# Attention sums of two query blocks in one session, and a head laid in another order, in a fused transformer block

## The chip, the cores and the metric

The kernel runs on one core of one Trainium2 chip. The metric is the device time of one execution in microseconds (us), the median of several runs; before the change it is 978.51 us over 3 runs. The engines are TensorE (PE; its weight loads are shown apart as PEld), VectorE (DVE), ScalarE (ACT), GpSimd (POOL) and SyncE (SP), which issues most transfers.

## The reference

One block of a transformer on x of 2048 tokens by 640 channels, in 32-bit floating point, whose norms are modulated by a condition c. Cut to what matters:

```python
mod = (_silu(c) @ w_mod).reshape(c.shape[0], 6, 1, -1)
sa, ca, ga, sb, cb, gb = (mod[:, i] for i in range(6))
h = _layernorm(x) * (1 + ca) + sa
x = x + ga * attention(h, wqkv, wo)        # 32 heads of 20, causal, window of 256 tokens
h = _layernorm(x) * (1 + cb) + sb
x = x + gb * mlp(h)                        # layernorm, 640 -> 1536, gelu, 1536 -> 640
```

A query sees the 256 keys up to and with its own, so in blocks of 128 tokens a query block meets three key blocks: its own and the one two back are masked to a triangle, the one between is whole.

## The kernel before, in words

The large products (projections, wo, MLP) are made of three matmuls each: the operands are split into a high part that TensorE multiplies fast (fp32r) and a low part, the rest; high by high, low by high and high by low are added in PSUM. A w_hi is a copy, a w_lo or hlo a subtraction. One line of the profile covers nearly all instructions, L116, the helper that keeps them in the order in which they are written: every engine works its own list in program order, and waits where a semaphore says so.

**The head** goes up to the first scores. It loads c (as columns, and as a row spread over all partitions, silr), x of the first 512 tokens (xs0), the first weights, the 640 columns' modulation weights wc in five pairs, x of the next 512 (xs1), the table sel and the constant rows of two key buffers (ones_k). All of these are issued on SP's queue, in that order but for the place of xs1 between the second and third pair. Then ORDER, a string, lays out the work: T turns a tile of 128 channels of a chunk of 512 tokens (transposes on TensorE, modulation and high part on ACT), L makes its low part (on POOL if it is in LOWP, else on DVE), P does its six matmuls, M computes a column pair of the modulation (sa, ca): on TensorE if it is in PE_COLS, else by eight multiply-and-sum operations on DVE and three small ones. S are statistics of a block of xs1, N normalizes xs1, R are matmuls without use that keep TensorE going, RUN0 as many ahead of all, E evacuates a product, Y lays it into the score buffers.

**The attention loop** has one iteration t for each of 128 score items (2 halves of the tokens, 8 quads of four heads, 8 query blocks) and some more to drain. In iteration t, TensorE does in this order: the exponent's scores e of the item 11 iterations back (LAG; keys by queries), the scores s of item t (queries by keys, for the row maximum), the sums o (exponent times v) of the query block that is due, and then a share of the projections pp that a planner has laid into four slots of the iteration, with asides (transposes, small sums) between. DVE masks e, masks s and takes its maximum nm; ACT copies the sums from PSUM (oT), takes the exponent pt; POOL makes the two triangular parts of pt by masking copies. The sums of a query block lie PVLAG iterations behind the e that completes it. ACT's queue then stores each second oT to o_scr. The sums, the turned tiles and the other asides share one PSUM bank, tag o.

The planner lay_units spreads the matmuls of 54 projection units over the iterations up to 108: an even room for each, less what else the iteration holds, where EXTRA[t] shifts the running total at t by so many matmuls. EARLY, AFTER, SUMS_LAST, WHOLE and the lists of times place single steps. From about iteration 115 on the blocks of 128 tokens that are done go through mid_steps: o scaled and split, wo, the first residual, the norm, its modulation, the transposes for the MLP. norm1 applies mean and deviation on ACT, mod multiplies by cb and adds sb in two halves, on DVE or on POOL. The rest of the blocks is done inside the MLP that follows.

What the steps touch: pv_stage, pv_copy and pv_store (the sums), pv_at (where they lie), lay_units, norm1 and mod in mid_steps, turned_in and modulate in the head, and the loads ahead of ORDER.

Of the kernel before, what the change touches and what calls it, by code (L numbers as in the profile page):

```python
# [31 lines left out]
PVLAG = 2  # L32
RUN0 = 33
PE_COLS = (0, 2)
PARTS = 4
MODV = 133
WOL = [1, 1, 0, 0, 0]
ORDER = ('T00 M1 L00 S0 S1 S2 T01 R8 S3 L01 P00 R5 N M2 R4 T02 M3 P01 T03 R2 L02 R1 T10 L10 L03 R6 C T11 M4 P02 T04 L11 P10 L04 T12 L12 T13 P03 P11 P04 L13 E0 T14 L14 Y00 P12 P13 Y01 P14')
LOWP = ['L00', 'L11', 'L03', 'L10', 'L13', 'L12', 'L04']
# [29 lines left out]
MODS = [[8.75, 17.0], [18.75, 27.0], [70.25, 79.0]]
WOS = [89.75, 94.0, 99.5, 109.0, 111.75, 114.25, 117.5]  # L70
W1S = [117.75, 121.75, 133.75]
RS = [[79.5, 82.5], [86.0, 87.0]]
# [1420 lines left out]
```

## Time and profile before

| What | us |
|---|---|
| Three runs | 977.36, 978.51, 978.64 |
| Median | 978.51 |
| Span of the profiled execution, first to last instruction | 975.4 |
| TensorE busy in it | 945.9 (97%) |
| DVE, ACT, POOL busy | 589.0, 445.1, 487.8 |
| First scores, start of the attention loop's work | 48.5 |

For the profiled execution the page gives its span; the time of the runs includes 2.0 to 3.2 us that lie outside it, by the difference. A row of a group of instructions reads: line, engine, operation, output <- inputs, shapes, count, then busy time and the mean of one in ns, then idle time of the engine ahead of them and what ended it. A row of a timeline reads: start, length, engine, line, operation, tiles, shapes, count. Matmuls are pipelined and their ends are modelled, so of two in a row the distance of the starts tells what one costs.

### The profile page before, as it was taken

How to read it: one execution, taken by the hardware profiler on the slowest of the kernel's cores; microseconds unless marked ns; L12 is line 12 of the kernel's file. 1: busy time of each engine (PE TensorE's matmuls, PEld its weight loads, DVE VectorE, ACT ScalarE, POOL GpSimd, SP SyncE). 2: the span in 40 equal slices, each digit the busy share in tenths (PEclk: the TensorE clock that was granted, in tenths of full speed). 3: DMA queues.
4: the chain of work that ended last, by engine and by line, in shares of the span. 5: the costliest groups of instructions: out<-in, count | busy, mean ns of one | idle time of the engine just before them, and what ended most of it. 6: DMA issues, size and time to landing. Idle time of an engine off the chain costs nothing.

```text
span 975.4 us, 20091 instructions
## 1 busy us (share of the span) xinstructions
PE 945.9 (97%) x7781; PEld 751.9 (77%) x7781; DVE 589.0 (60%) x991; ACT 445.1 (46%) x781; POOL 487.8 (50%) x674
## 2 busy tenths in 40 slices
PE   8899999999999999999889999999999999999998
PEld 8777777777777777777677677888888888888886
DVE  6564977888776786767788556563544344342112
ACT  3723555666654545555545654434333243333222
POOL 3423555677864364463646844654454454332121
PEclk9999999999999999999999999999999999999999
DMA  8366778666778359854862245444413342124113
GB/s 307 97 210 197 244 228 274 188 187 170 220 226 251 114 175 283 240 157 120 226 161 76 81 142 156 127 130 138 138 57 103 115 145 85 54 58 144 54 43 119
DMA packets 98974, 152.17 MB, mean 156 GB/s; under 512 B 8864, under 2 KB 42112, under 8 KB 98880
## 3 DMA queue, kind: packets, MB, share of 16 engines
q1 hardware_dynamic: 89664, 142.50, 48.4%
q10 hardware_dynamic: 9216, 8.39, 2.7%
q8 instruction: 62, 1.02, 0.4%
q14 instruction: 32, 0.26, 0.1%
HBM read 98.51 MB, written 51.58 MB: 154 GB/s over the span
## 4 chain that ended last, share of the span: by engine, by line
PE 81%; DVE 7%; ACT 5%; DMA 2%; issue 2%; POOL 1%; SPq 1%; ACTq 0%; DVEq 0%; POOLq 0%
PE pp L116 17%; PE out L116 16%; PE h L116 16%; PE e L116 8%; PE o L116 7%; PE wo L116 6%; PE s L116 4%; ACT pt L116 3%; DVE e L116 2%; PE ppo L116 1%; SPq L116 1%; PE yt L116 1%; DVE nm L116 1%; DMA wc<-in_wcol 1%; PE xt L116 1%
## 5 line engine op out<-in xcount | busy, mean ns | idle before, releaser
L116 POOL TENSOR_SCALAR_AFFINE_SELECT pt<-pt 128x512 f32<-128x512 f32 x192 | 129.1, 672 | 128.8 <-ACT pt L116 122.0
L116 ACT ACTIVATE pt<-e 128x1024 f32<-128x1024 f32 (+1 forms) x120 | 133.7, 1114 | 64.5 <-DVE e L116 62.0
L116 DVE TENSOR_REDUCE nm<-s 128x1 f32<-128x256 f32 (+4 forms) x206 | 157.6, 796 | 4.4
L116 POOL TENSOR_TENSOR w2lo<-w2r,w2hi 128x640 fp32r<-128x640 f32 x48 | 78.5, 1635 | 163.0 <-ACT w2hi L116 163.0
L116 PE MATMUL e<-qbuf,kbuf 62*128 62x128 f32 (+2 forms) x773 | 111.8, 328 | 10.6 <-ACT pt L116 9.5
L116 DVE CAST ghi<-g 128x512 fp32r<-128x512 f32 x48 | 27.4, 571 | 155.0 <-ACT g L116 155.0
L116 PEld LDWEIGHTS e<-qbuf,kbuf 62*128 62x128 f32 x773 | 80.8, 185 | 49.8 <-ACT pt L116 25.9
L116 PE MATMUL pp<-hhi,w_hi 128*128 128x512 f32 x265 | 113.6, 429 | 0.2 <-ACT pf L116 0.2
L116 PE MATMUL s<-kbuf,qbuf 60*128 60x384 f32 (+2 forms) x728 | 105.9, 302 | 4.3 <-DVE nm L116 1.9
L116 PE MATMUL pp<-hlo,w_hi 128*128 128x512 f32 x265 | 108.3, 409 | 0.6 <-POOL hlo L116 0.6
L116 DVE COPY_PREDICATED e<-mask_t,e 128x512 f32<-128x512 uint32 x96 | 66.6, 694 | 70.0 <-PE e L116 65.8
L116 PE MATMUL pp<-hhi,w_lo 128*128 128x512 f32 x265 | 106.2, 401 | 0.0
L116 PE MATMUL o<-pt,vbuf 128*32 128x128 f32 x2688 | 99.6, 277 | 0.6 <-ACT xT L116 0.6
L116 PEld LDWEIGHTS s<-kbuf,qbuf 60*128 60x128 f32 x728 | 89.1, 186 | 14.2 <-DVE nm L116 5.9
L116 PE MATMUL out<-ghi,w2hi 128*128 128x512 f32 x240 | 95.3, 397 | 0.9 <-ACT g L116 0.9
L116 PE MATMUL out<-glo,w2hi 128*128 128x512 f32 x240 | 93.9, 391 | 0.0
L116 PE MATMUL out<-ghi,w2lo 128*128 128x512 f32 x240 | 93.8, 391 | 0.0
L116 POOL TENSOR_TENSOR w_lo<-wraw,w_hi 128x128 fp32r<-128x128 f32 x171 | 76.1, 476 | 31.4 <-ACT w_hi L116 31.4
L116 PE MATMUL h<-yhi,w1hi 128*128 128x512 f32 x220 | 87.6, 398 | 0.0
L116 PE MATMUL h<-ylo,w1hi 128*128 128x512 f32 x220 | 86.1, 392 | 0.0
L116 PE MATMUL h<-yhi,w1lo 128*128 128x512 f32 x220 | 86.0, 391 | 0.0
L116 DVE COPY_PREDICATED s<-mask_t,s 128x512 f32<-128x512 uint32 x112 | 77.1, 688 | 13.8 <-PE s L116 13.5
(179 smaller groups left out, 1838.3 us busy)
## 6 DMA issues: line engine op xcount, KB each, us to landing
w2r<-in_w SPq DMA_DIRECT2D x48, 320.0 KB
qbuf<-q_scr SPq DMA_DIRECT2D x60, 240.0 KB
wraw<-in_wqkv SPq DMA_DIRECT2D x36, 320.0 KB
kbuf<-k_scr SPq DMA_DIRECT2D x44, 240.0 KB
q_scr<-stage SPq DMA_DIRECT2D x20, 512.0 KB
k_scr<-stage SPq DMA_DIRECT2D x20, 512.0 KB
o_scr<-oT ACTq DMA_DIRECT2D x64, 128.0 KB
wm<-in_wmod SPq DMA_DIRECT2D x20, 320.0 KB
```

What stands on the lines that cost most here:

```text
L116: return self.tc.keep_in_program_order(op(*args, **kw))
```

## The change: what it does

Sums: pv_stage does two query blocks in one session, into one bank as two columns blocks; one copy brings both to SBUF and one store follows. A pair b of a quad lies at u = min(2b + 1, 6) + half, one iteration (PVLAG = 1) behind its last e, so that in eight iterations four have sums, where each had before. SPOT names iterations whose sums are done in a later slot, behind projections. The planner counts PV_COST = 2 matmuls for an iteration with sums, and EXTRA has other values.

Head: x's tiles are asked for first; c goes on ACT's queue; the stores of constant rows come ahead of the last column pairs; LOADS is the order. M1 joins M0 and M2 on TensorE, RUN0 goes from 33 to 21, the R entries from 26 in sum to 1. ORDER, LOWP and HIGHV (high parts on DVE instead of ACT) are laid anew.

Second norm: norm1 goes; mod works on all 640 columns, first (x - mean) times cb, then times the deviation plus sb, both on DVE. WLV names units whose next weights' low parts are made on DVE instead of POOL.

UNITS, LNS, LOV, HIA, EARLY, AFTER, SUMS_LAST, WHOLE, MODS, WOS, W1S, RS, WARM, LATE_AT, TAIL0, TAIL_AT, MID_AT and CHAIN have some other values (CHAIN without norm1), which the diff leaves out.

```diff
-PVLAG = 2
-RUN0 = 33
-PE_COLS = (0, 2)
+PVLAG = 1
+RUN0 = 21
+PE_COLS = (0, 1, 2)
...
-MODV = 133
-ORDER = ('T00 M1 L00 S0 S1 S2 T01 R8 S3 L01 P00 R5 N M2 R4 T02 M3 P01 T03 R2 L02 R1 T10 L10 L03 R6 C T11 M4 P02 T04 L11 P10 L04 T12 L12 T13 P03 P11 P04 L13 E0 T14 L14 Y00 P12 P13 Y01 P14')
-LOWP = ['L00', 'L11', 'L03', 'L10', 'L13', 'L12', 'L04']
+ORDER = 'T00 L00 S0 M1 T01 S1 L01 S2 R1 P00 S3 M2 T02 N M3 P01 T03 T10 L02 L10 C L03 T11 M4 T04 P02 L04 P10 T13 T12 P03 P04 L11 P11 E0 L12 L13 Y00 T14 P12 L14 Y01 P13 P14'
+LOADS = 'x0 x1 c1 x3 x2 w1 r0 w0 m0 m1 y0 y1 o m2 m3 s m4'
+HIGHV = ['H03', 'H13', 'H14', 'H12']
+LOWP = ['L00', 'L10', 'L01', 'L03', 'L02', 'L12']
...
-MV = [8, 9, 12, 17, 19, 21, 22, 26, 28, 29, 30]
+WLV = [0, 12, 14, 15, 18, 28, 29, 33, 47, 49, 57, 59]
+SPOT = {99: 3, 40: 3, 44: 3, 128: 2, 115: 1, 118: 1, 69: 2, 54: 3, 119: 3, 107: 3, 11: 3, 45: 3, 51: 3, 14: 2, 109: 1, 123: 2, 111: 3, 89: 3, 76: 3}
...
+PV_COST = 2.0
-EXTRA = {9: -2, 10: -3, 11: 5, 14: -4, 15: 3, 16: -4, 17: 2, 18: 1, 19: -3, 20: -4, 21: 6, 22: 1, 23: 1, 25: 4, 26: -3, 27: 3, 28: -3, 29: 7, 30: -5, 31: 1, 32: -3, 33: -1, 34: -1, 35: -3, 36: 3, 37: 9, 38: -8, 39: 3, 40: -3, 41: -8, 42: -2, 43: 3, 44: -3, 45: 9, 46: 3, 47: -1, 48: 4, 50: 1, 51: -3, 52: -16, 53: 7, 54: -5, 55: 4, 56: -7, 57: 13, 58: -1, 59: 10, 60: -1, 61: 3, 63: 2, 64: -1, 65: 10, 66: -4, 67: -1, 69: 2, 70: -4, 71: 4, 72: 3, 73: 3, 75: -9, 76: -2, 77: -3, 78: -1, 79: -1, 80: -4, 81: -9, 82: 15, 83: 6, 84: -2, 85: 2, 86: 2, 87: 11, 88: 4, 89: -9, 90: 3, 91: 1, 92: 3, 93: -6, 94: -12, 95: 1, 96: 1, 98: 3, 99: 2, 100: 2, 101: 7, 102: -3, 103: 6, 104: -4, 105: -1, 106: -6, 107: -2, 108: -1, 109: 7, 110: 1, 111: 3, 112: 4, 114: -1}
+EXTRA = {50: -4, 53: 3, 42: -4, 57: 2, 58: -6, 47: -8, 52: 4, 20: 3, 21: -4, 77: 3, 78: -4, 54: 4, 89: 9, 91: -2, 112: 7, 113: -1, 19: -1, 103: 1, 106: 2, 9: -3, 48: 10, 49: -3, 29: 2, 85: 6, 86: -5, 56: -1, 34: -6, 36: 2, 35: 9, 67: 8, 68: -5, 41: 2, 11: 1, 10: -2, 27: 1, 24: -4, 75: 13, 88: -4, 114: 1, 84: -1, 62: 1, 87: -2, 105: -1, 80: -5, 61: 7, 14: 1, 15: -1, 8: 1, 30: 3, 66: -2, 45: 8, 46: -7, 96: -1, 93: -1, 104: -4, 90: -3, 117: -5, 118: 6, 120: -1, 108: -3, 111: -6, 73: -11, 76: 1, 101: 5, 110: 1, 37: -7, 33: 2, 18: 1, 17: -1, 38: 4, 115: 8, 25: 2, 39: -1, 69: -4, 72: 4, 107: -1, 92: 2, 63: 1, 116: -5, 83: -1, 102: -3, 32: -3, 95: 1, 94: -4, 81: 3, 70: 1, 71: -1, 22: 1, 40: 2, 65: -1, 26: -3, 100: 1, 59: 1}
...
-    def pv_stage(half, quad, qb):
+    def pv_stage(half, quad, b):
         q = quads[half, quad]
-        ob = pools["o"].tile([P, P], F32, tag="o", name=f"o{half}_{quad}_{qb}")
-        kbs = [kb for kb in range(qb - 2, qb + 1) if (kb, qb) in q["p"]]
-        for kb in kbs:
-            v = vblk(half, quad, kb)
-            pt, col = q["p"][kb, qb]
-            for i, h in enumerate(HEADS):
-                matmul(
-                    ob[32 * h : 32 * h + 32], v[:, h * VW : h * VW + 32], pt[:, i, col : col + P],
-                    start=kb == kbs[0], stop=kb == kbs[-1], tile_position=(0, 32 * h), skip_group_check=True,
-                )
+        ob = pools["o"].tile([P, 2, P], F32, tag="o", name=f"o{half}_{quad}_{b}")
+        for c in range(2):
+            qb = 2 * b + c
+            kbs = [kb for kb in range(qb - 2, qb + 1) if (kb, qb) in q["p"]]
+            for kb in kbs:
+                v = vblk(half, quad, kb)
+                pt, col = q["p"][kb, qb]
+                for i, h in enumerate(HEADS):
+                    matmul(
+                        ob[32 * h : 32 * h + 32, c], v[:, h * VW : h * VW + 32], pt[:, i, col : col + P],
+                        start=kb == kbs[0], stop=kb == kbs[-1], tile_position=(0, 32 * h), skip_group_check=True,
+                    )
         return ob
-    def pv_copy(half, quad, qb, ob):
+    def pv_copy(half, quad, b, ob):
         q = quads[half, quad]
-        b, c = divmod(qb, 2)
-        if c == 0:
-            q["oT"] = att.tile([P, 2, P], F32, tag="oT", bufs=2, name=f"oT{half}_{quad}_{b}")
-        nc.scalar.copy(q["oT"][:, c], ob)
-        if qb == NQB - 1:
+        q["oT"] = att.tile([P, 2, P], F32, tag="oT", bufs=2, name=f"oT{half}_{quad}_{b}")
+        nc.scalar.copy(q["oT"], ob)
+        if b == NQB // 2 - 1:
             done_v.add(half * QUADS + quad)
-    def pv_store(half, quad, qb):
-        b, c = divmod(qb, 2)
-        if c:
-            t0 = half * HALF + b * 256
-            nc.scalar.dma_start(o_scr[quad * 4 : quad * 4 + 4, :, t0 : t0 + 256], quads[half, quad]["oT"].rearrange("p c t -> p (c t)"))
+    def pv_store(half, quad, b):
+        t0 = half * HALF + b * 256
+        nc.scalar.dma_start(o_scr[quad * 4 : quad * 4 + 4, :, t0 : t0 + 256], quads[half, quad]["oT"].rearrange("p c t -> p (c t)"))
...
+            if nm == "a":
+                bx[nm] = mv[:, 0:1], rs
+                return
             nr = mid.tile([P, 1], F32, tag="nr", bufs=3, name=f"nr{nm}{bg}")
             nc.gpsimd.tensor_tensor(nr, mv[:, 0:1], rs, ALU.mult)
             nc.gpsimd.tensor_scalar(nr, nr, -1.0, None, ALU.mult)
             bx[nm] = nr, rs
-        def apply_(dst, src, nm):
-            nr, rs = bx[nm]
-            nc.scalar.activation(dst, src, AF.Identity, bias=nr, scale=rs)
-
-        def norm1():
-            bx["y"] = box2["mid"].tile([P, D], F32, tag="yb", name=f"y{bg}")
-            apply_(bx["y"], bx["x"], "a")
+        def norm2():
+            nr, rs = bx["b"]
+            nc.scalar.activation(bx["y"], bx["y"], AF.Identity, bias=nr, scale=rs)
         def mod(h):
-            y, cs = bx["y"][:, 320 * h : 320 * h + 320], slice(320 * h, 320 * h + 320)
-            eng = nc.vector if now[0] >= MODV and bg < len(TAIL0) or 2 * bg + h in MV else nc.gpsimd
-            eng.tensor_tensor(y, y, box2["cb"][:, cs], ALU.mult)
-            eng.tensor_tensor(y, y, box2["sb"][:, cs], ALU.add)
+            mean, rs = bx["a"]
+            if h == 0:
+                bx["y"] = box2["mid"].tile([P, D], F32, tag="yb", name=f"y{bg}")
+                nc.vector.scalar_tensor_tensor(bx["y"], bx["x"], mean, box2["cb"], ALU.subtract, ALU.mult)
+            else:
+                nc.vector.scalar_tensor_tensor(bx["y"], bx["y"], rs, box2["sb"], ALU.mult, ALU.add)
...
-    nc.sync.dma_start(c_sb, c)
     silr = base.tile([P, D], F32, tag="acc", name="silr")
-    nc.sync.dma_start(silr, crow.to_broadcast([P, D]))
-    xs0 = ln1_load(0)
-    nc.scalar.activation(sil, c_sb, AF.Silu)
-    nc.scalar.activation(silr, silr, AF.Silu)
-
+    xs0 = [base.tile([P, D], F32, tag="xt", bufs=4, name=f"xt0_{b}") for b in range(4)]
     wc = [[prj.tile([P, 2, CHUNK], F32, tag="stage", bufs=4, name=f"wc{j}{g}").rearrange("p a n -> p (a n)")[:, 0:D] for g in range(2)] for j in range(2)]
     flat = vcar.rearrange("p q b v -> p (q b v)")[:, 0 : 2 * D].rearrange("p (g d) -> p g d", d=D)
     wc.append([flat[:, g] for g in range(2)])
         for g in range(2):
             nc.sync.dma_start(wc[j][g], wcol[j, g])
-    w_load(0, 0, 0)
-    w_load(0, 1, 0)
-    wc_load(0)
-    wc_load(1)
     xs1 = []
-    for b in range(0, 4, 2):
-        xt = att.tile([P, 2, D], F32, tag="pt", bufs=NPT, name=f"xs1_{b}")
-        t0 = CHUNK + b * P
-        nc.sync.dma_start(xt, x[t0 : t0 + 2 * P, :].rearrange("(b p) d -> p b d", p=P))
+    xp = [att.tile([P, 2, D], F32, tag="pt", bufs=NPT, name=f"xs1_{b}") for b in range(2)]
+    for xt in xp:
         xs1 += [xt[:, 0], xt[:, 1]]
-    for j in range(2, KT):
-        wc_load(j)
-
     sel_t = kb_[NSLOT - 1].rearrange("p a n -> p (a n)")
     sel_raw = att.tile([P, 8 * P], F32, tag="pt", bufs=NPT, name="sel_raw")
-    nc.sync.dma_start(sel_raw, sel)
-    ones_k(range(NSLOT - 1))
+
+    def load_x1(b):
+        t0 = CHUNK + 2 * b * P
+        nc.sync.dma_start(xp[b], x[t0 : t0 + 2 * P, :].rearrange("(b p) d -> p b d", p=P))
+
+    for op in LOADS.split():
+        k = int(op[1:] or 0)
+        if op[0] == "c":
+            (nc.sync, nc.scalar)[k].dma_start(c_sb, c)
+            nc.scalar.activation(sil, c_sb, AF.Silu)
+        elif op[0] == "r":
+            (nc.sync, nc.scalar)[k].dma_start(silr, crow.to_broadcast([P, D]))
+            nc.scalar.activation(silr, silr, AF.Silu)
+        elif op[0] == "x":
+            nc.sync.dma_start(xs0[k], x[k * P : (k + 1) * P, :])
+        elif op[0] == "y":
+            load_x1(k)
+        elif op[0] == "w":
+            w_load(0, k, 0)
+        elif op[0] == "m":
+            wc_load(k)
+        elif op[0] == "s":
+            nc.sync.dma_start(sel_raw, sel)
+        else:
+            ones_k(range(NSLOT - 1))
...
-        nc.scalar.copy(hT[ch][0][:, kt], hf)
+        (nc.vector.tensor_copy if f"H{ch}{kt}" in HIGHV else nc.scalar.copy)(hT[ch][0][:, kt], hf)
...
+    pv_at = {}
+    for half in range(2):
+        for quad in range(QUADS):
+            for b in range(NQB // 2):
+                u = min(2 * b + 1, 6) + half
+                pv_at.setdefault(LAG + PVLAG + (half * QUADS + quad) * NQB + u, []).append((half, quad, b))
     def lay_units(room):
         used, act = collections.Counter(), collections.Counter()
         for t in asides:
             used[t] += 0.5
+        for t in pv_at:
+            used[t] += PV_COST
...
-                    put(*divmod(ends[1 if kt < 2 else 2], 4), lambda nxt=nxt, kt=kt: w_lo(nxt, kt, gp))
+                    put(*divmod(ends[1 if kt < 2 else 2], 4), lambda nxt=nxt, kt=kt, eng=nc.vector if i in WLV else gp: w_lo(nxt, kt, eng))
...
-        sums = [(*key, pv_stage(*key)) for key in pv_at.get(t, ())]
+        sums = [] if t in SPOT else [(*key, pv_stage(*key)) for key in pv_at.get(t, ())]
...
+            if SPOT.get(t) == h:
+                for key in pv_at.get(t, ()):
+                    pv_copy(*key, pv_stage(*key))
```

More of the change, by code (lines that the diff above doesn't have):

```diff
@@ L65 @@
+AFTER = {0: 2, 2: 2, 4: 3, 5: 2, 6: 1, 7: 1, 8: 2, 9: 1, 10: 2, 11: 2, 12: 1, 14: 2, 15: 1, 19: 1, 20: 1, 21: 2, 22: 1, 23: 2, 27: 1, 32: 1, 34: 1, 35: 1, 36: 1, 38: 3, 39: 6, 40: 2, 41: 1, 43: 1, 47: 1, 48: 1, 45: 3, 42: 2, 51: 4, 59: 2, 60: 1, 17: 2, 18: 1}
+SUMS_LAST = [14, 15, 19, 26, 29, 35, 42, 43, 50, 59, 63, 64, 71, 74, 76, 79, 83, 86, 87, 88, 89, 90, 91, 92, 93, 105, 106, 107, 108, 110, 111, 113, 114, 116, 117, 118, 120, 121, 122, 123, 126, 130, 131, 132, 133, 135, 136, 139]
 LEAST = 4
@@ L66 @@
 CUT = 3
-WHOLE = [11, 12, 23, 24, 26, 28, 29, 31, 38, 39, 40, 42, 43, 44, 45, 47, 50, 53, 55, 57, 60, 63, 75, 76, 84, 86, 90, 108, 109, 111, 112, 115, 116, 121, 122, 124, 125, 126, 127]
+WHOLE = [11, 12, 17, 23, 24, 25, 26, 28, 31, 38, 39, 40, 43, 44, 45, 47, 50, 53, 55, 57, 63, 75, 76, 78, 84, 86, 87, 90, 106, 109, 111, 122, 124, 126, 127]
 MOST = 10
[L69 to L72, printed above, removed]
+MODS = [[7.5, 16.0], [17.75, 27.5], [67.75, 79.0]]
@@ L73 @@
+WOS = [90.25, 93.5, 100.5, 109.25, 113.0, 113.25, 117.5]
+W1S = [117.5, 123.75, 133.5]
+RS = [[76.0, 79.5], [82.25, 85.0]]
 TOMID = 109
-WARM = {(115, 0): 2, (121, 0): 2, (127, 2): 1, (130, 1): 4, (135, 0): 5, (136, 0): 10}
-LATE_AT = [105.75, 106.5, 106.75, 108.75, 110.25, 111, 113.25]
-TAIL0 = [115.25, 120.25, 124.25, 129.25]
+WARM = {(115, 0): 3, (121, 0): 1, (127, 2): 3, (130, 1): 1, (135, 0): 5, (136, 0): 10, (129, 1): 1}
+LATE_AT = [106.0, 106.0, 107.0, 108.5, 109.75, 110.75, 114.25]
+TAIL0 = [115.25, 120.25, 124.25, 128.75]
@@ L929, in mid_steps @@
             "load": load, "om": o_scale, "oh": o_high, "ol": o_low, "add0": w0[KT], "add1": w1_[KT],
-            "sa0": lambda: stats(bx["x"], "a", 0), "sa1": lambda: stats(bx["x"], "a", 1), "n1": norm1,
+            "sa0": lambda: stats(bx["x"], "a", 0), "sa1": lambda: stats(bx["x"], "a", 1),
             "m0": lambda: mod(0), "m1": lambda: mod(1), "x0": xtrans(0, 4), "x1": xtrans(4, KT),
             "sb0": lambda: stats(bx["y"], "b", 0), "sb1": lambda: stats(bx["y"], "b", 1),
-            "n2": lambda: apply_(bx["y"], bx["y"], "b"), "y0": y0, "y0l": y0_low, "y1": y1, "y1l": y1_low,
+            "n2": norm2, "y0": y0, "y0l": y0_low, "y1": y1, "y1l": y1_low,
         }
@@ L1301, in block_kernel @@
     n = len(s_items)
-    pv_at = {}
-    for half in range(2):
-        for quad in range(QUADS):
-            for qb in range(NQB):
-                pv_at.setdefault(LAG + PVLAG + (half * QUADS + quad) * NQB + qb + half, []).append((half, quad, qb))
     for t in range(n + LAG + PVLAG + 4):
```

18 lines of the change are left out of this document (8 added, 10 removed).

## The prediction

> **What bounds the kernel now.** I read the page's totals first, then the busy time by stretches.
>
> ```profile
> span 975.4 us, 20091 instructions
> ...
> PE 945.9 (97%) x7781; PEld 751.9 (77%) x7781; DVE 589.0 (60%) x991; ACT 445.1 (46%) x781; POOL 487.8 (50%) x674
> ```
>
> TensorE is busy for 97% of the span, and no other engine is above 60%. So a microsecond counts if TensorE's stream gets shorter by it, or if a wait of TensorE goes. The stretches (columns: length, then busy time of PE, PEld, DVE, ACT, POOL with the number of instructions, granted clock, DMA) tell where waits are left:
>
> ```profile
> 400.00:500.00 100.00, 94.08 (x1151) 70.96 (x1155) 74.26 (x106) 53.45 (x105) 53.09 (x71) 1.00 0.61 170
> 500.00:580.00 80.00, 73.76 (x981) 58.72 (x980) 57.13 (x104) 47.49 (x81) 53.36 (x80) 1.00 0.37 106
> 580.00:975.40 395.40, 389.63 (x1888) 328.11 (x1886) 164.07 (x295) 131.32 (x209) 164.16 (x167) 1.00 0.34 106
> ```
>
> After 580 us (the MLP) TensorE idles 5.8 us in 395, and the change gives it the same matmuls: I cost that stage at nothing. Between 400 and 580 it idles 180 - 167.8 = 12.2 us, in the late attention loop. Everything below is therefore about the loop and about the head, which ends with the first scores at 48.5 us.
>
> **Part 1, the sums of two blocks in one session.** A session is the group of small matmuls (tile o) between the scores and the projections of an iteration. From TensorE's timeline (start, duration, count):
>
> ```profile
> 104.89 0.42 PE L116 MATMUL o<-pt,vbuf 128*32 128x128 f32 x8
> 105.25 0.50 PE L116 MATMUL pp<-hlo,w_hi 128*128 128x512 f32 x1
> ...
> 108.03 0.35 PE L116 MATMUL s<-kbuf,qbuf 60*128 60x256 f32 x2
> 108.30 0.64 PE L116 MATMUL o<-pt,vbuf 128*32 128x128 f32 x16
> 108.88 0.50 PE L116 MATMUL pp<-hhi,w_hi 128*128 128x512 f32 x1
> ...
> 112.05 0.86 PE L116 MATMUL o<-pt,vbuf 128*32 128x128 f32 x24
> 112.84 0.50 PE L116 MATMUL pp<-hlo,w_hi 128*128 128x512 f32 x1
> ```
>
> From the first o to the next projection a session of 8 takes 0.36 us, of 16 takes 0.58, of 24 takes 0.79. That is 0.14 us once, and 0.22 us for every 8 matmuls. The matmuls stay (two blocks of 24 become 48); one fixed part in two goes: 2 x 0.79 - (0.14 + 6 x 0.2165) = 0.14 us a pair. Does the iteration without a session pay something in its place? It goes from the scores straight to projections, as before iteration 11:
>
> ```profile
> 71.98 0.62 PE L116 MATMUL s<-kbuf,qbuf 60*128 60x384 f32 x4
> 72.53 0.50 PE L116 MATMUL ppo<-hhi,w_hi 128*128 128x512 f32 x1
> ```
>
> The projection starts 0.07 us ahead of the scores' modelled end (72.60); in the session at 108.30 it is 0.08 us ahead (108.38). Leaving the scores costs the same either way, so nothing is taken off or put on. 16 quads of four pairs make 64 pairs: 64 x 0.14 = **-9.0 us**. Bounds: 0, if the second block begins as a session of its own (the trace has none of 48), and -26, if the iteration without sums also saved the step from scores to session (108.03 to 108.30, 0.27 us). I take the slope, since three lengths lie on it.
>
> [...]
>
> SPOT lists 19 iterations in which the sums are moved behind some projections. With the new lag, sums lie at iterations 13, 15, 17, 18 and every 8 on in the first half, at 78, 80, 82, 83 and every 8 on in the second; of the 19 only 45, 69, 99, 107, 115, 118, 123 and 128 carry any. Each then enters from projections and leaves to them, one change more, which I price like the fixed part: 8 x 0.14 = **+1.1 us** (bounds 0 and 8 x 0.27 = 2.2).
>
> **Part 2, the lag of one iteration.** PVLAG falls from 2 to 1 and a pair waits for its second block, so a session comes one iteration behind the exponentials of its last key block. What must be done by then is exponent (ACT), two triangular masks (POOL). One item of before, with the session that lies where the new one would (173 us), and then a late one:
>
> ```profile
> 170.22 1.03 ACT L116 ACTIVATE pt<-e 128x1024 f32<-128x1024 f32 x1
> ...
> 171.32 1.34 POOL L116 TENSOR_SCALAR_AFFINE_SELECT pt<-pt 128x512 f32<-128x512 f32 x2 [2.60 <-ACT pt L116]
> ...
> 172.76 0.64 PE L116 MATMUL o<-pt,vbuf 128*32 128x128 f32 x16
> ```
>
> ```profile
> 260.92 0.86 PE L116 MATMUL o<-pt,vbuf 128*32 128x128 f32 x24
> ...
> 261.23 1.54 POOL L116 TENSOR_SCALAR_AFFINE_SELECT pt<-pt 128x512 f32<-128x512 f32 x2
> ```
>
> The first is masked at 172.66, 0.10 us before TensorE is there. The second is masked at 262.77 behind other POOL work, 1.85 us after the session at 260.92 began. And an iteration without a session is 0.79 us shorter, while the planner's PV_COST of 2 in four of eight iterations gives it only one projection matmul more (0.23 us, from 3.47 us for 15 in the head, below). So with an even schedule most masked sessions would be late by 0.79 - 0.23 - 0.10 = 0.46 us. Against it stand the new EXTRA values, which shift projections into the iterations ahead of a session (iteration 20: 3 - (-1) = +4 matmuls, before -4 - (-3) = -1; each is worth 0.23 us), and WLV, which takes w_lo off POOL. I take **+1.0 us** in all, between 0 and the rival below.
>
> Waiting behind a late session in TensorE's queue are the iteration's projections and then the next e, so the stall is whole. The copies of the sums and their stores on ACT's queue come half as often, and the bank that sessions share with turned tiles is held half as often. TensorE's waits between 400 and 580 us:
>
> ```profile
> PE e L116 <- ACT pt L116: 7.7, 11, 2.0
> PE pm L116 <- ACT oT L116: 1.1, 1, 1.1
> PE yt L116 <- ACT oT L116: 0.9, 2, 0.5
> PE pv L116 <- ACT oT L116: 0.7, 1, 0.7
> ```
>
> The last three are waits for that bank, 2.7 us; half of it is **-1.3 us** (bounds 0 and -2.7). The first I leave, see the rivals.
>
> **Part 3, the modulation after the first norm, and w_lo on DVE.** norm1 goes, and two DVE operations of 640 columns stand for four of 320.
>
> ```profile
> L116 DVE SCALAR_TENSOR_TENSOR acc<-wm,sil,acc 128x640 f32<-128x640 f32 x12 | 12.6, 1050 | 0.0
> ...
> L116 DVE TENSOR_TENSOR y<-y,sb_b 128x320 f32<-128x320 f32 x13 | 12.1, 934 | 0.4
> ...
> L116 DVE TENSOR_TENSOR w_lo<-wraw,w_hi 128x128 fp32r<-128x128 f32 x5 | 1.1, 281 | 0.0
> ```
>
> The nearest row of that form is 1.05 us, so 2.1 us of DVE for each of 16 blocks, 33.6 us, for some 24 us that it did before (13 halves, each two operations of about 0.9); w_lo adds 5 x 0.281 = 1.4 us at each of at most twelve places. DVE was at 74 of 100 us in the late loop and at 164 of 395 after it: I cost this at **0**, hidden under TensorE. If that cover is gone the s maximum and the e mask are late, which is the first rival's mechanism again.
>
> **Part 4, the head.** The chain that ended last, in order of time (start, duration):
>
> ```profile
> 4.72 7.43 DMA wc<-in_wcol
> ...
> 12.29 2.38 PE psm L116 x20
> ...
> 17.80 1.30 DVE wc L116
> ...
> 19.73 0.81 DVE st L116 x2
> ...
> 24.17 1.34 POOL rs L116
> ...
> 29.31 0.79 ACT hf L116
> ...
> 36.18 3.47 PE pp L116 x15
> ...
> 48.48 0.44 PE s L116 x4
> ```
>
> After column 0 (TensorE, to 14.67) DVE works on column 1 until 19.73, then on the statistics of the second chunk, then POOL takes the root, then DVE normalizes and does column 3, then ACT can go on. With column 1 on TensorE (20 more small matmuls, 2.38 us by column 0, in place of warm-up matmuls), DVE reaches the statistics at about 15 us: up to 4.8 us earlier. Of that I keep **-3.0 us**: x of the second chunk is asked for behind two columns' loads, as before, and need not be there at 15 us; the root waits on POOL behind w_lo and two hlo, since L01 is now POOL's; and the second chunk's products then run as densely as TensorE can. x asked for first skips two issues on SP's queue, 0.9 us, but the columns come behind the same bytes, so that it moves the chain's first row by at most that; it is in the 3.0. The four constant stores on SP's queue now stand ahead of columns 2 to 4: they are wanted only from about 20 us on. Bounds: 0 and -5.7 (4.8 + 0.9).
>
> **The sum**: -9.0 + 1.1 + 1.0 - 1.3 - 3.0 = -11.2 us. It is made against the profiled span of 975.4; the median of the runs, 978.5, is 3.1 above it (head and end outside the span), which I carry over unchanged: 978.5 - 11.2 = **967.3 us**. Its own range is 961 to 973.
>
> **The rivals.** *Sums come too early for the masks* (slower). The 44 masked sessions that SPOT doesn't move (three in four of 64, less 4) each wait the 0.46 us worked out above: 20.2 us, in place of my 1.0: **986.5 us**. For it: the late item above; against it: EXTRA and a freer POOL. It decides from (11.2 + 1.0) / 44 = 0.28 us each on. Chance 0.12.
>
> *The clock falls in the head.* Columns on TensorE are matmuls of one column:
>
> ```profile
> 12.05:15.46 3.41, 3.17 (x28) 3.08 (x29) 2.58 (x8) 1.94 (x4) 3.41 (x7) 1.00 1.04 396
> 15.46:18.88 3.42, 3.42 (x20) 3.42 (x17) 3.42 (x11) 1.22 (x2) 3.42 (x6) 0.50 1.04 396
> ```
>
> In 12.05 to 15.46 TensorE did only the columns of the chain's row at 12.29 and transposes, busy for 3.17 of 3.41 us, and in the next stretch the granted clock was 0.50. The change adds another column there and drops most warm-up (33 to 21, and 26 to 1 later). Two more such stretches under dense products cost 2 x 3.41 / 2 = 3.4 us, the whole gain of the head: **970.7 us**, chance 0.13. [...]
>
> *The waits for the exponent go too*: ACT is rid of norm1 and half of the copies, and the 7.7 us above go: **959.6 us**, chance 0.12. Against it: they end with DVE's mask more than with ACT's queue, and DVE gets more to do.
>
> *A session of 48 is two of 24*: the fixed part stays, 967.3 + 9.0 = **976.3 us**, chance 0.06. My own case has the remaining 0.57.
>
> **Chances and range.** A change under 0.2% (2.0 us) can't be told from none here, so faster is below 976.5 and slower above 980.5. My case, the clock and the exponent lie below (0.82), half of the fourth (0.03) and the mildest first (0.01): 0.86. Same is 0.05, from the fourth and a half-hidden first; slower the rest of the first, 0.09. The range runs from 958 (the third, nearly whole) to 976 (just below the fourth); the first is what it leaves out.
>
> **What would show it.** Sessions of 48 taking 1.4 to 1.5 us from first o to the next projection, and 64 of them; the first s at 45 to 46 us instead of 48.5; waits of o for POOL's pt summing to about 1 us; idle TensorE between 400 and 580 us not above 12. I am wrong if o waits for pt by tens of microseconds, if a session of 48 takes 1.58, or if the granted clock shows 0.50 in two stretches between 15 and 40 us.

## The result, and the profile after

The changed kernel takes **985.36 us** (four runs: 980.88, 984.45, 986.27, 986.99) against 978.45 us of the kernel before beside it: ratio 1.0066, 95% interval 1.0049 to 1.0084. It is slower by 0.7%, where 967.3 us was forecast. The profile is of the run of 980.88, the fastest of the four. One run of experiment 14 below took 1286.40 us at a mean granted clock of 0.653 and counts in no ratio here. The page's totals:

```profile
span 979.1 us, 19756 instructions
...
PE 941.5 (96%) x7727; PEld 755.2 (77%) x7727; DVE 607.3 (62%) x1015; ACT 424.5 (43%) x702; POOL 439.8 (45%) x581
```

The span is 3.7 us longer than before, with TensorE busy 4.4 us less: idle time grew by 8.1 us. The part that was to save time did save it. Here is a session of two blocks on TensorE's timeline, and the page's group of all sums, first of the changed kernel and then of the one before:

```profile
486.90 1.52 PE L119 MATMUL o<-pt,vbuf 128*32 128x128 f32 x48
488.35 0.50 PE L119 MATMUL pp_late<-hhi,w_lo 128*128 128x512 f32 x1
...
L119 PE MATMUL o<-pt,vbuf 128*32 128x128 f32 x2688 | 88.6, 275 | 0.8 <-ACT pt L119 0.6
```

```profile
L116 PE MATMUL o<-pt,vbuf 128*32 128x128 f32 x2688 | 99.6, 277 | 0.6 <-ACT xT L116 0.6
```

From the first o to the next projection 1.45 us, as the slope of the three short sessions gave (1.44). The same 2688 matmuls keep TensorE busy 11.0 us less. With 192 more that read vcar in place of vbuf, they come as 56 sessions of 48 and 8 of 24, and they wait 0.6 us in all for exponents: the sums are not too early.

So the time went elsewhere. The stretches that the prediction read (length, busy PE, PEld, DVE, ACT, POOL, granted clock, DMA), changed kernel:

```profile
400.00:500.00 100.00, 93.57 (x1136) 71.51 (x1124) 76.01 (x116) 51.97 (x90) 47.59 (x59) 1.00 0.64 183
500.00:580.00 80.00, 70.98 (x970) 57.24 (x970) 63.29 (x108) 40.31 (x61) 43.35 (x60) 1.00 0.37 105
580.00:975.40 395.40, 394.87 (x1919) 333.03 (x1917) 170.85 (x304) 124.70 (x202) 135.55 (x118) 1.00 0.35 106
```

Between 400 and 580 us TensorE idles 15.4 us instead of 12.2, although the sums are shorter. From 50 to 400 us, a stretch that the prediction left out, it is busy 340.24 us instead of 344.10 and so idles 9.8 us instead of 5.9. From 580 us to the end it idles 4.2 us instead of 5.8, and in both kernels 3.7 of these lie behind its last matmul. TensorE's waits from 48 us to the end of the loop, changed kernel (line waited for: us in total, times, longest):

```profile
PE e L119 <- ACT pt L119: 11.0, 26, 1.2
PE e L119 <- DMA qbuf<-mlo: 2.5, 1, 2.5
PE wo L119 <- POOL ot_lo L119: 1.8, 3, 0.7
PE s L119 <- DMA kbuf<-k_scr: 1.6, 1, 1.6
```

and before:

```profile
PE e L116 <- ACT pt L116: 9.5, 16, 2.0
...
PE wo L116 <- POOL ot_lo L116: 0.3, 1, 0.3
```

Two waits for transfers are new, mlo and k_scr; the prediction names neither. A third place is the head. TensorE's timeline there, changed kernel:

```profile
11.32 3.08 PE L119 MATMUL psm<-sil,wc 128*128 128x1 f32 x20 [2.81 <-DMA wc<-in_wcol]
...
15.15 4.26 PE L119 MATMUL psm<-sil,wc 128*128 128x1 f32 x20
...
20.45 0.78 PE L119 MATMUL pp<-hhi,w_hi 128*128 128x512 f32 x1
...
23.10 2.36 PE L119 MATMUL psm<-sil,vcar 128*128 128x1 f32 x20
```

The second column takes 4.26 us of TensorE, and the stretches of the head say why (the first row ends where the clock falls):

```profile
9.36:12.77 3.41, 1.45 (x13) 1.48 (x14) 1.21 (x3) 3.11 (x5) 2.20 (x5) 1.00 1.03 410
...
12.80:16.20 3.40, 3.40 (x18) 3.40 (x18) 1.07 (x4) 1.36 (x2) 2.77 (x7) 0.50 1.04 393
16.20:19.60 3.40, 3.40 (x18) 3.40 (x18) 0.39 (x5) 0.62 (x1) 1.26 (x1) 0.50 0.87 165
19.60:23.00 3.40, 3.40 (x12) 2.65 (x10) 3.18 (x12) 1.40 (x2) 1.08 (x1) 0.50 0.98 275
23.00:26.40 3.40, 3.40 (x28) 3.25 (x28) 1.12 (x6) 0.36 (x1) 1.21 (x2) 1.00 1.01 390
26.40:29.80 3.40, 3.40 (x13) 2.30 (x11) 3.40 (x18) 2.68 (x4) 1.39 (x1) 0.50 0.33 127
```

Half clock in four stretches, where before there was one. TensorE is full in all five from 12.80 us on, VectorE in two of them (3.18 and 3.40 of 3.40 us). In the stretch ahead of the first fall TensorE is busy for only 1.45 of 3.41 us: the warm matmuls end at 8.51 us, and then it waits 2.81 us for the first column's weights. The first scores start at 49.6 us instead of 48.5.

### The profile page after: what moved, and what is told of

Read it like the earlier page. It is cut to its first block, busy times and chain, and to the rows that moved or that the text cites. A ratio compares the mean times of both kernels' runs of the same rounds, so it can differ in the third digit from the quotient of the medians.

```text
span 979.1 us, 19756 instructions
## 1 busy us (share of the span) xinstructions
PE 941.5 (96%) x7727; PEld 755.2 (77%) x7727; DVE 607.3 (62%) x1015; ACT 424.5 (43%) x702; POOL 439.8 (45%) x581
## 5 line engine op out<-in xcount | busy, mean ns | idle before, releaser
L119 DVE TENSOR_REDUCE nm<-s 128x1 f32<-128x256 f32 (+5 forms) x210 | 157.7, 784 | 4.4
L119 DVE CAST ghi<-g 128x512 fp32r<-128x512 f32 x48 | 24.5, 509 | 158.2 <-ACT g L119 158.2
L119 PE MATMUL pp<-hhi,w_hi 128*128 128x512 f32 x265 | 115.8, 437 | 1.6 <-ACT pf L119 0.6
L119 PEld LDWEIGHTS s<-kbuf,qbuf 60*128 60x128 f32 x728 | 88.9, 186 | 16.4 <-DVE nm L119 6.7
L119 PE MATMUL o<-pt,vbuf 128*32 128x128 f32 x2688 | 88.6, 275 | 0.8 <-ACT pt L119 0.6
L119 POOL TENSOR_TENSOR w_lo<-wraw,w_hi 128x128 fp32r<-128x128 f32 x146 | 63.9, 467 | 43.6 <-ACT w_hi L119 43.5
```

The costliest lines, as they stand in the source:

```text
L119: return self.tc.keep_in_program_order(op(*args, **kw))
```

## The experiments

Kernels of one batch share their runs of the kernel before; ratios are to those. "Old head" means LOADS, ORDER, LOWP, HIGHV, RUN0 and PE_COLS as before.

**1. The head undone.** The changed kernel with the old head:

```diff
-RUN0 = 21
-PE_COLS = (0, 1, 2)
+RUN0 = 33
+PE_COLS = (0, 2)
...
-LOADS = 'x0 x1 c1 x3 x2 w1 r0 w0 m0 m1 y0 y1 o m2 m3 s m4'
...
+LOADS = 'c0 r0 x0 x1 x2 x3 w0 w1 m0 m1 y0 y1 m2 m3 m4 s o'
```

> The changed kernel with the head of before (loads in the old order, ORDER, LOWP, PE_COLS, RUN0 as before, no high parts on DVE); the loop and the rest as changed. Theory, the head's clock: the changed head runs 13 to 30 us at half clock, differently in each run, and that is most of the loss and all of the spread. Then the first scores are back at 48.5 us, the granted clock is 0.50 in one stretch of the head only, the time falls from 985.4 to 979 to 982 us and the runs agree within 1.5 us. Rival, the loop alone is slower: the time stays within 2 us of 985 and the runs still lie 5 us apart.

981.12 us, ratio 1.0036 [1.0020, 1.0052]; the first scores at 48.5 us. The new head is a loss (1.0066 against 1.0036), though the two intervals meet. More than half of what is lost remains, and the runs still lie 3.6 us apart (979.88 to 983.46). This profile, of the slowest run, also shows something that the profiled run of the changed kernel does not, half clock in the middle of the loop:

```profile
482.70:489.50 6.80, 4.27 (x68) 3.05 (x66) 5.37 (x8) 3.96 (x5) 4.63 (x6) 1.00 0.32 89
489.50:496.30 6.80, 6.33 (x69) 5.41 (x69) 3.90 (x5) 1.45 (x1) 0.24 (x1) 0.50 0.47 128
```

A stretch in which TensorE is busy 4.27 of 6.80 us is followed by one at 0.50. In that stretch lies the wait for mlo. The same wait in the profiled run of the changed kernel, in a stretch as little busy, is not followed by half clock:

```profile
483.80:490.60 6.80, 4.39 (x68) 3.12 (x67) 5.47 (x8) 3.95 (x5) 4.67 (x6) 1.00 0.32 84
490.60:497.40 6.80, 5.58 (x87) 4.76 (x87) 4.79 (x7) 2.49 (x4) 1.44 (x2) 1.00 0.52 154
```

**2. Warm matmuls again**, in the new order:

```diff
-RUN0 = 21
+RUN0 = 33
-ORDER = 'T00 L00 S0 M1 T01 S1 L01 S2 R1 P00 S3 M2 T02 N M3 P01 T03 T10 ...
+ORDER = 'T00 R8 L00 S0 M1 R8 T01 S1 L01 S2 R1 P00 R5 S3 M2 R4 T02 N M3 P01 T03 R2 T10 R6 ...
```

> The changed kernel with warm-up matmuls put back into the new head: 33 ahead instead of 21, and 8, 8, 5, 4, 2 and 6 between the columns, transposes and products. Theory, the clock: fewer stretches at 0.50, first scores at 46 to 48 us instead of 49.6, time 977 to 981 us, runs within 2 us. Rival, the head is late through the order of its transfers (columns 2 to 4 behind the constant stores): first scores at 49.5 us or later, time 983 to 987.

982.14 us, 1.0048 [1.0031, 1.0064]. The clock is at half only from 19.2 to 22.7 us. TensorE waits 0.40 us for the first column instead of 2.81, and the fall at 12.8 us is gone:

```profile
9.01:12.42 3.41, 3.01 (x28) 2.85 (x27) 1.87 (x6) 2.65 (x4) 1.99 (x4) 1.00 1.03 403
```

So that fall comes with the warm matmuls that were dropped. But the first scores start later still, at 50.8 us: the warm matmuls stand ahead of transposes and columns in TensorE's list. Half clock is not the whole of the head's loss.

**3. The second tile's column back on VectorE**, in the new order (PE_COLS = (0, 2)):

> The changed kernel with column 1 back on DVE, nothing else. Theory, the clock falls because nothing dense runs on TensorE between 9 and 20 us, whoever makes the column: TensorE is even emptier, the clock shows 0.50 as long or longer, the time is 984 to 990 us. Rival, the one-column matmuls of column 1 themselves cost the head: time 979 to 982 us.

983.99 us, 1.0065 [1.0048, 1.0082]: no difference to the changed kernel. The first scores start at 50.8 us. TensorE waits 3.17 us for the first column, and the clock is at half from 13.1 to 30.1 us, longer than with the second column on TensorE: the half clock of the new head does not hang on that column. This run too has the fall of the clock in the loop, from 490.9 to 497.8 us, behind a stretch busy for 4.40 of 6.80 us.

**4. Pairs alone.** The kernel before with the new pv_stage, pv_copy, pv_store, pv_at and PVLAG = 1; EXTRA and all other lists as before:

> The kernel of before with one part of the change alone: the sums of two blocks in one session, one iteration behind (no SPOT, planner and tables of before). Theory, the loop gives the session's 9 us back in waits, because iterations with and without sums differ in length: waits of o for POOL's pt and of e for ACT's pt grow by 10 us or more, time 978 to 988 us. Rival, the pairs are a gain and other edits lose it: time 968 to 972 us.

1000.14 us, 1.0229 [1.0213, 1.0245]. The sessions are as short as in the changed kernel, and the rest loses more than twice that:

```profile
PE e L116 <- ACT pt L116: 16.0, 30, 1.8
PE s L116 <- DVE nm L116: 2.4, 10, 0.3
...
PE o L116 <- POOL pt L116: 1.5, 2, 0.9
```

With the lists of before, pairs are a loss. It is of the size of the prediction's first rival, but not its mechanism: the sums wait 1.5 us for their masks, while the scores wait for exponents and maxima. Against the kernel before, the distances of the starts in the loop grew by 7.0 us from a projection to the next e, by 6.8 from e to s and by 5.8 from s to s.

**5 and 6. The two transfers.** WOS lists when the tiles of wo are scaled, UNITS the order of the projections. First WOS of before in the changed kernel:

```diff
-WOS = [90.25, 93.5, 100.5, 109.25, 113.0, 113.25, 117.5]
+WOS = [89.75, 94.0, 99.5, 109.0, 111.75, 114.25, 117.5]
```

> The changed kernel with one list of times as before, WOS (the scaling of wo on POOL, whose last step in the changed kernel ends 1.5 iterations later). Theory, a transfer wait: the load of r waits on SP's queue for the tile that this scaling reads, the maxima's rows (mlo) stand behind it, TensorE waits 2.5 us for them at 489 us, and in most runs that pause also halves the clock for one or two stretches. Then the wait for mlo is gone, no 0.50 after 40 us in the granted clock, time 978 to 981 us, and the spread of the runs falls below 3 us. Rival, the spread is the head's: time 983 to 985, spread 5.

981.15 us, 1.0033 [1.0020, 1.0046], and the wait for mlo is gone: this list alone is worth 0.33%, 3.2 us, in the changed kernel. The half clock that was to go with it did not: the profile has it from 515.4 to 522.2 us, behind a stretch busy for 5.42 of 6.90 us, and the runs lie 3.5 us apart. Then old head, old WOS and old UNITS (k1 ahead of v0 again) together:

> The changed kernel with the head of before, WOS of before, and UNITS of before (v after k again, so that the first k rows reach the scratch earlier). Theory, two transfer waits: 2.5 us (mlo) and 1.7 us (kbuf from k_scr at 86 us) go, and the half clock in the loop with them: 974 to 977 us. Rival, the waits hide others and nothing comes of it: 979 to 981.

976.84 us, 0.9993 [0.9984, 1.0003]: even with the kernel before. Against experiment 1 the two lists are worth 0.43%, 4.2 us. Their mechanism, that of WOS above all, shows on the queue of SyncE in the changed kernel, and then in the timelines of GpSimd and TensorE:

```profile
477.51 0.67 SPq L119 DMA_DIRECT2D ob<-o_scr  x1
486.06 0.55 SPq L119 DMA_DIRECT2D r<-r_scr  x1
...
487.34 0.58 SPq L119 DMA_DIRECT2D qbuf<-mhi  x1
487.97 0.54 SPq L119 DMA_DIRECT2D qbuf<-mlo  x1
```

```profile
484.50 1.53 POOL L119 TENSOR_TENSOR wor<-wor,ga_b 128x640 f32<-128x640 f32 x1
...
491.39 0.52 PE L119 MATMUL e<-qbuf,kbuf 62*128 62x128 f32 x5 [2.53 <-DMA qbuf<-mlo]
```

The load of r takes the buffer (tag acc) in which the last scaling of wo reads ga_b. That scaling ends at 486.03, so SyncE's queue stands from 478 to 486, and the rows of the maxima, which only happen to be queued behind, reach TensorE 2.5 us late. In experiment 6 the same load goes out at 478.97, and the maxima are asked for some 6 us earlier:

```profile
478.97 0.56 SPq L119 DMA_DIRECT2D r<-r_scr  x1
...
481.82 0.55 SPq L119 DMA_DIRECT2D qbuf<-mlo  x1
```

There the granted clock was 1.00 in each of three stretches from 480 to 500.4 us, and 0.998 in the mean of the run. In experiment 1 the two waits are 2.3 and 1.8 us, and in 6 a wait of 0.7 us for k_scr is left, so that waits of 3.4 us went, against 4.2 us gained. The mean granted clock rose as well, from 0.991 to 0.995 in the runs of 1 to 0.996 to 1.000 in those of 6; what of the 4.2 us is due to the clock was not separated.

The runs of the changed kernel differ in the same way: 980.88 us at a mean granted clock of 0.993, 984.45 at 0.987, 986.27 and 986.99 at 0.984. By these means the profiled run was at half clock for 14 us, as its profile shows, and the others for 26 to 32 us (an estimate: twice the missing share of the span). So the profile that is read above has the least half clock of the four, and of the 6.9 us that the median lost, the 4.5 us between that run and the median go with half clock that this profile does not show.

In the loop a fall of the clock came behind a stretch busy for 63% with one pause of 2.3 us (experiment 1) and behind one busy for 79% (5), and did not come behind one busy for 65% with a pause of 2.5 us (changed kernel), so these runs give no busy share that decides. The half clock lasted 6.8 us each time: from 489.5 to 496.3 and from 516.8 to 523.6 us in experiment 1, from 515.4 to 522.2 in 5.

**7. Even iterations.** My reading then was that iterations without sums are too short for the exponents. Experiment 6 with a higher price of a session, so that the planner moves projections out of the iterations with sums:

```diff
-PV_COST = 2.0
+PV_COST = 5.0
```

> As the kernel before it, and the planner counts a session as 5 matmuls instead of 2, so that iterations with sums get fewer projections and those without get more. Theory, uneven lengths: iterations without sums (3.47 us against 4.19) wait for the exponent and for the row maximum, and at even length these waits fall by 3 us or more: 971 to 974 us. Rival, the tables (EXTRA) had evened them out and are now put out of step: 976 to 982.

987.88 us, 1.0108 [1.0090, 1.0126], and TensorE's waits for exponents rose from 12.0 to 16.4 us. The theory fell, though the test is weak: the matmuls of projections in an iteration with sums went only from 5.3 to 4.9 on average in the iterations up to 108 (LEAST keeps four), and EXTRA, tuned for the other price, no longer fits.

**8 and 9. The second norm.** Its modulation as before in experiment 6, with norm1 and the times that belong to it, and, the reverse, as changed in the kernel before. The core of the first:

```diff
-                nc.vector.scalar_tensor_tensor(bx["y"], bx["x"], mean, box2["cb"], ALU.subtract, ALU.mult)
...
-                nc.vector.scalar_tensor_tensor(bx["y"], bx["y"], rs, box2["sb"], ALU.mult, ALU.add)
+            eng.tensor_tensor(y, y, box2["cb"][:, cs], ALU.mult)
+            eng.tensor_tensor(y, y, box2["sb"][:, cs], ALU.add)
```

> As the kernel before the last (old head, two waits taken away), and the second norm's modulation as before: norm1 on ACT, mod in halves on DVE or POOL. Theory, that part is hidden under TensorE: within 1 us of the kernel with two waits taken away. Rival, DVE's two operations of 640 columns keep the e mask waiting in the last iterations: 2 to 4 us faster.

> The kernel before with one part of the change alone: the modulation of the second norm by two operations on VectorE (subtract mean, times column; times root, plus row), without the first-norm activation on ScalarE and the four operations on GpSimd or VectorE per block; everything else is the kernel before's. Theory (this part was a gain by itself that the prediction put at nothing): 0.8 to 1.8 us less, ratio 0.9982 to 0.9992. Rival (it gained only where the sums are in pairs, because VectorE and GpSimd stand differently there): within 0.4 us, ratio 0.9996 to 1.0004.

Without it experiment 6 is at 1.0007 [0.9998, 1.0017], so with it 0.14% better, though the intervals meet; alone in the kernel before it is 1.0017 [1.0008, 1.0026], worse. Neither the theory nor the rival of the second run had that sign. The part has no single price: it is worth some 1.5 us either way, by the kernel around it. The granted clock tells the two apart. Of the runs at 0.998 or more, those without the part take 976.8 to 977.2 us and those of experiment 6 976.6 to 977.2, so its gain there goes with falls of the clock. In the second run's profile the clock also fell in the loop, behind a stretch busy for 4.06 of 6.80 us, but its two runs at 0.998 or more still take 978.0 and 978.6 us, against 976.1 to 977.4 for the kernel before: that loss is not the clock alone.

**10 and 11. The head's two named parts, each alone in experiment 6.** x asked for first (LOADS = 'x0 x1 c1 r0 x3 x2 w0 w1 m0 m1 y0 y1 m2 m3 m4 s o'), and the column on TensorE (PE_COLS = (0, 1, 2)):

> The kernel with the old head and without the two waits of the loop, and in it only the order of the loads is new: x0 and x1 asked for first, c on ScalarE's queue, the row of c after them; columns, order of TensorE's work and warm matmuls as in the kernel before. Theory (in the head VectorE's sums of columns set the pace, not the landing of x): the first statistics start 2 to 3 us earlier, the first score matmul stays within 0.4 us of 48.3, time within 0.4 us of the same kernel without this (0.9993 of before). Rival (x is what the head waits for): first score matmul 1 to 3 us earlier and the time 1 to 3 us less (ratio 0.996 to 0.998). Third way (the row of c comes too late for the sums of columns): first score matmul 0.5 to 2 us later.

> The kernel with pairs, old head and without the two waits of the loop, and in it the second tile's modulation columns on TensorE instead of VectorE, nothing else of the new head. If VectorE's sums set the head's pace, as the prediction had it: VectorE is free 2.4 to 4.8 us earlier, first score matmul at 44 to 46.5 instead of 48.3, time 2 to 4 us less. Rival (the root and the copies of the columns still wait their turn, and TensorE's 40 one-column matmuls stand in front of the transposes): first score matmul within 0.7 us of 48.3 or later, time within 0.7 us of the same kernel without it.

x first: 976.57 us, 0.9993 [0.9984, 1.0002], no change against experiment 6. The first statistics start at 3.93 us (6.80 in the kernel before), the first scores at 48.2 instead of 48.3. x was not what the head waited for. This is the fastest of all versions, and it can't be told from the kernel before. The column on TensorE: 979.14 us, 1.0006 [0.9997, 1.0014], 0.13% more than without, at the edge of what the intervals resolve, and the first scores at 50.1. The 2 to 4 us of gain are ruled out. TensorE's timeline with it:

```profile
15.03 4.19 PE L119 MATMUL psm<-sil,wc 128*128 128x1 f32 x20
19.08 1.09 PE L119 MATMUL psx<-idn,xt 128*128 128x128 f32 x4
19.97 2.97 PE L119 MATMUL warm<-idn 128*128 128x128 f32 x16
22.70 0.48 PE L119 MATMUL pp<-hhi,w_hi 128*128 128x512 f32 x1
```

and in experiment 6 without it:

```profile
14.40 1.14 PE L119 MATMUL psx<-idn,xt 128*128 128x128 f32 x8
15.38 3.18 PE L119 MATMUL warm<-idn 128*128 128x128 f32 x16
18.21 0.77 PE L119 MATMUL pp<-hhi,w_hi 128*128 128x512 f32 x1
```

The first product moves from 18.21 to 22.70 us, by 4.5 us, of which the column is 4.2. In both, TensorE works without a gap from 14.5 us until past 27 us, in part on warm matmuls, so there the order and length of TensorE's list set the pace, and VectorE is relieved of work that was hidden.

**12 and 13. A dose of TensorE's time.** The first matmul of each projection in the loop is done twice, in the kernel before and in experiment 6:

```diff
+                if i == 0 and not acc:
+                    matmul(box["ps"], w[:, kt], h[:, kt], start=True, stop=True)
                 matmul(box["ps"], w[:, kt], h[:, kt], start=i == 0, stop=i == 3 * KT - 1)
```

> The kernel before, with the first matmul of each projection in the loop (those that use the projection bank, about 49) done twice, 0.23 us each: 11.4 us of TensorE's time added in the loop, nothing else. If the loop is TensorE's own work throughout: 10.5 to 11.8 us more, ratio 1.0107 to 1.0121. If part of the iterations end with the wait for the exponents and take it in: the difference, 7 to 10 us more.

> The same doubling, 11.4 us of TensorE's time, in the kernel with sums of two query blocks, old head and without the two waits of the loop. Theory (the iterations without sums wait for the exponents and maxima, and so the time that the shared session saves comes back there): clearly less than in the kernel before, 4 to 8 us more against the same kernel without it, ratio to before 1.003 to 1.0075. Rival (the loop is as much bound by TensorE's work with pairs as without): the same cost as in the kernel before, 10 to 11.8 us, ratio 1.0095 to 1.0115.

985.32 us, 1.0082 [1.0069, 1.0096], and 984.60 us, 1.0075 [1.0061, 1.0089]: 8.0 us in each for 11.4 us of work (0.82% and 0.75 + 0.07%). My theory, that with pairs the loop takes it in, fell. In both, a microsecond of TensorE's work that is added in the loop costs 0.7 us (0.6 to 0.8 by the intervals). By the two traces with pairs, the iterations with sums that hold an added matmul grew by 0.18 us for each, those without sums by 0.20: the latter have no more spare time than the former.

**14 and 15. The order on ScalarE.** In experiment 6 ScalarE is idle ahead of 40 copies of sums until the session ends, with the exponents behind it in its list. The view of that tile, by what its engine waited for:

```profile
L119 ACT COPY oT<-o x64: 357/372/375, 105.6 to 575.5; 128x256 f32<-128x256 f32 x64
...
  PE o L119: 68.3, 40
```

In these two the copies always stand behind the exponents (SUMS_LAST holds every iteration), with pairs and, as the control, in the kernel before:

> The kernel with pairs, old head and without the two waits of the loop, and in it the copy of the sums (oT) always behind the exponents on ScalarE, not in the 48 listed iterations only. In the profile ScalarE sits idle ahead of 40 of the 64 copies for 68 us in all, 1.7 us each, until the session of 48 ends, and the exponents stand behind it. Theory (that is where the session's gain goes: a longer session holds the exponents back, and the next scores with them): TensorE's waits for the exponents in the loop fall from 12 us to under 8 and the time falls by 2 to 5 us, ratio to before 0.994 to 0.997. Rival (the exponents are not late by that, and the bank of the sums now comes free 1.1 us later for the side work that shares it): waits of TensorE for the copy rise by 2 us or more, time 1 to 5 us more, ratio 1.000 to 1.005.

> The control: the kernel before with the copies of the sums always behind the exponents. There 80 of 128 copies stand ahead of them, with 108 us of idle ScalarE, 1.35 us each. If the order on ScalarE decides in general: the same sign and about the same size as with pairs. If it is the longer session that makes it matter: no change or slower here, ratio 1.000 to 1.006, and a gain with pairs.

983.59 us, 1.0055 [1.0041, 1.0068], and 997.80 us, 1.0200 [1.0184, 1.0217]. TensorE's waits in the first:

```profile
PE e L119 <- ACT pt L119: 12.5, 23, 1.2
PE psx L119 <- ACT oT L119: 2.6, 3, 1.1
```

The matmuls' wait for exponents stays at 12 us (the weight loads' falls, from 31.2 to 25.4), and the side work waits for the bank instead. In the control the waits for the exponent fall from 9.5 to 6.9 us, but those for the bank rise from 3.2 to 19.6, about what the kernel loses. The idle time of ScalarE was no loss: the theory fell, and the bank of the sums is the scarcer thing, in both kernels.

## Why the prediction was wrong, point by point

By the ratios, in shares of 978 us: the head +2.9 us (1.0066 to 1.0036), the two lists +4.2 (1.0036 to 0.9993), all the rest -0.7. The first two are good to about 2 us each, by the intervals. The forecast had -3.0, nothing, and -8.2. The first rival's time, 986.5, lies near the measured 985.36 by luck, as its mechanism did not come.

- **Sessions, -9.0: right.** 1.45 us against 1.44, and 11.0 us less busy time. Leaving the scores for a projection costs as much as leaving them for a session, as assumed: in experiment 6 the median of either step is 0.27 us.
- **Lag, +1.0, SPOT, +1.1, and the first rival.** The changed kernel's sums wait 0.6 us, so the lag was priced well, and the rival's mechanism didn't come. SPOT was not measured by itself: no run shows what one change more costs. The bank's waits for copies of sums (-1.3) went from 2.7 us to 1.5 (0.9 for xt, 0.6 for pm): right.
- **"A microsecond counts if TensorE's stream gets shorter by it", and of the waits for the exponent "The first I leave": wrong**, and the step that failed for the 7.5 us between -8.2 and -0.7. First, the rate: the dose says that a microsecond counts 0.7 in the loop, so that 10.7 us (the sessions with the step that follows each, from start to start) should have been worth some 7.5, an estimate. That explains about 3 us of the miss. Second, the other steps didn't stay as they were. In experiment 6, from the first scores to the first matmul of the MLP, it takes 529.8 us against 528.4, so the other steps grew by 12.1 us, the whole saving and 1.4 more. Between the starts, those among the scores (e and s) grew by 4.0 us in sum, from a projection to the next scores by 3.5, from the scores to what follows by 3.2, wo to wo by 2.1, into a session from elsewhere by 1.3; the rest fell by 2.0. The waits for exponents in that kernel, and then in the one before, were not left as they were:

```profile
PE e L119 <- ACT pt L119: 12.0, 26, 1.2
...
PEld e L119 <- ACT pt L119: 31.2, 54, 1.4
```

```profile
PEld e L116 <- ACT pt L116: 25.9, 48, 2.3
```

For the matmuls that is 12.0 us against 9.5, for the weight loads (PEld) 31.2 against 25.9. In the late loop alone, from which the prediction took its row, the waits of the changed kernel's matmuls fell (6.3 us against 7.7); before 400 us they rose (4.7 against 1.8). The step into the next scores takes 0.48 us on average behind an iteration without sums in experiment 6, and 0.39 behind one with sums; in the kernel before it takes 0.43 behind one with sums. What makes these steps later has no single cause that the runs could show: it is not slack in the iterations without sums (13) nor the order of copies and exponents (14), and 7 was too weak to say whether an even spread would help. How far the lists can move it, experiment 4 shows: 22 us. This stays open.
- **UNITS and WOS costed at nothing: wrong**, 4.2 us. They were in the lists left out of the sum, without a reason given. SyncE's queue in the kernel before has the load of r in front of the maxima's rows too, but there it goes out at 479.20 us and the maxima come in time; the prediction did not look at it, nor at what the new WOS would do to it.
- **Second norm at 0:** between -1.4 and +1.7 us by the neighbours; the 0 lies between them by luck, and is no rule.
- **Head, -3.0: wrong in sign.** The failed step is "DVE reaches the statistics at about 15 us: up to 4.8 us earlier. Of that I keep -3.0". It followed the chain that ended last, in which VectorE has the rows at 17.80 and 19.73, and took what VectorE is rid of as time won. TensorE has no gap from 14.4 us until past 27 (experiment 6), partly with warm matmuls, and the column's 20 matmuls, priced at 2.38 us, take 4.2 at half clock and stand in front of the first product. The column alone costs 0.13%, 1.3 us; the other 1.6 us of the head lie in the order and the clock and were not split. The second rival, the clock, did come, in four stretches, one more than it said. The first of them comes with the warm matmuls that were dropped (experiment 2), not with the columns. It had set its price against a gain that was not there.
- **The 3.1 us between the profiled span and the median** are not all time outside the span, as the sum says: in every run its own span is 1.7 to 2.2 us below its time, and the rest is that the profiled run was a faster one. It was carried over unchanged and moved nothing.

Two of the tells held, the length of the sessions and the small wait for the masks. Three spoke against the forecast: 49.6 us to the first scores, 15.4 us of idle TensorE between 400 and 580, and 0.50 in more than two stretches of the head.

## What to carry to other kernels

A saved microsecond of the busiest engine counts only as long as every other step keeps its time; measure the exchange rate by adding a known amount of work before counting on taking some away. Treat each list of places and due times in a change as an edit with a price, and look through the in-order queues for a load that waits for a buffer, with something urgent behind it. Before work is moved to the bound engine to relieve another, check with that work alone that the other one was the bound. Where runs of one kernel lie apart, read the granted clock of each before taking the profiled one as typical.

## What the runs showed of the hardware

In two runs a pause of 2.3 to 2.4 us, in a stretch that was busy for 63 to 65%, was followed by TensorE's half clock for 6.8 us (experiments 1 and 3); in a third run a pause of 2.5 us in a stretch busy for 65% was not (changed kernel). In the head, 23.00 to 26.40 us of the changed kernel held 20 one-column matmuls, four transposes and a few products, and was followed by 0.50 although TensorE counted as busy throughout. A matmul of 320 columns took 0.31 us with fp32r operands (wo) and 0.43 with 32-bit ones (pmr), both in the kernel before. One multiply-and-sum of VectorE took 0.32 us, and 1.39 us where GpSimd ran a subtraction of low parts beside it (changed kernel):

```profile
27.74 1.39 DVE L119 CUSTOM_DVE_ANT_0 vbuf<-vbuf,silr 128x160 f32<-128x160 f32 x1
...
29.06 0.32 DVE L119 CUSTOM_DVE_ANT_0 vbuf<-vbuf,silr 128x160 f32<-128x160 f32 x1
```

```profile
27.55 1.39 POOL L119 TENSOR_TENSOR hlo<-hf,hhi 128x512 fp32r<-128x512 f32 x1 [3.17 <-ACT hhi L119]
```
